# Last-keys operand of 96 rows, a theta tail of eight matmuls, softmax sums with a gap, and copies moved to ScalarE

## The chip, the cores and the metric

The kernel runs on one core of a Trainium2 chip. The metric is the device time of one execution in microseconds. Five engines have a queue of instructions each and run beside one another: TensorE (PE, with its weight loader PEld), VectorE (DVE), ScalarE (ACT), GpSimd (POOL) and SyncE (SP), which here issues the DMAs.

## The reference

```python
# attention: B, H, S, D = 8, 8, 576, 64; pool = 8; Sp = 72
k_p = k.reshape(B, H, Sp, pool, D).mean(axis=3)
v_p = v.reshape(B, H, Sp, pool, D).mean(axis=3)
scores = scale * np.matmul(q, k_p.transpose(0, 1, 3, 2))
scores = scores - np.max(scores, axis=-1, keepdims=True)
attn = np.exp(scores)
attn = attn / (np.sum(attn, axis=-1, keepdims=True) + 1e-09)
x = matmul(attn, v_p) -> (B, S, H * D)
# first mixer: x is (8, 576, 512)
theta = x @ w_theta
zr, zi = x * np.cos(theta), x * np.sin(theta)
y = einsum('ts,bsd->btd', w_tok_r, zr) + einsum('ts,bsd->btd', w_tok_i, zi)
u = x + y
x = u + np.maximum(u @ w_ch, 0.0)
# second mixer
h = np.maximum(x.transpose(0, 2, 1) @ w_tok1, 0.0) @ w_tok2
u = x + h.transpose(0, 2, 1)
out = u + np.maximum(u @ w_ch1, 0.0) @ w_ch2
```

## The kernel before

All is float32. Where a matmul runs in the float32r form, an operand is split into a hi part (a cast) and a lo part (what the cast lost), and hi·hi, hi·lo and lo·hi are added up in PSUM. PSUM has eight banks of 512 columns: two called m for the token mix, two called t for theta, four called x for scores, transposes and attention.

The prologue (to about 84 us) converts weights and does batch 0's attention. Then `interleave(mix_steps(b), side)` runs for b = 0 to 7: the token mix of batch b, 216 matmuls `m<-wtk,Z` in eight groups of 27, each group taken out by DVE at L789 (`R<-m,R`), and between them side steps for batch n = b + 1, the attention and theta that the next mix needs:

- `emit_sc`: scores, DVE's maximum (L552) and subtraction (L553), ACT's exp (L558);
- `emit_norm`, once for each of four pairs of heads p: DVE sums e (L564), adds 1e-9 and multiplies by 8 (L565), inverts (L568); POOL multiplies (L569) and copies the last eight of the 72 pooled keys of two heads into `pl` (L574);
- `emit_pt`: e transposed on PE (L173), 64 keys of two heads to a tile `pt`, the last eight keys of all heads to a tile `t`; ACT casts the hi part (L604, L608), DVE subtracts for the lo part (L605, L610);
- `emit_av`, for each of four pairs of heads j and two parts th of the tokens (256 and 320 columns): five matmuls into one x bank, three with `pt` (vbh, vbl, vbh) and two with the last keys (`vlh` of 128 rows and `vll`). ACT takes the result out twice (Xh L645, R L646), DVE subtracts (Xl L650);
- `dup_tail` (L536): the last 64 tokens of Xh, Xl and R (their chunk 4 is half full) are copied beside themselves, so that chunk 4 has 128 columns; the half that is copied gives the sine, the other the cosine;
- `emit_theta`: x @ w_theta into t banks, two halves (half) and chunks g; g = 2 is the tail, chunk 4, 12 matmuls of 512 columns (eight with Xh, four with Xl). ACT adds a constant that rounds (L705), DVE takes the fraction (L718), ACT takes the absolute value (L710, L714) and the sine (L711, L712, L715);
- `emit_z`: x transposed again, DVE multiplies (L736, L745), ACT casts (L750), POOL subtracts for the lo part (L751).

Keys, values and last values of later batches are loaded and summed in between: `prep_k` (sum over the pool of eight, L398, then two copies into the block-diagonal `bdk`, L403), `prep_v`, `prep_vl` (POOL builds vlh and vll from one 64-row sum by a mask).

The order is written by a planner: `mm` and `tp` count a clock of PE's columns, a table P gives each side step its due time on that clock within the mix, `later(dt, ...)` puts a follow-up dt behind, and `need` flushes what a tag still waits for. A scheduler then orders each engine's queue. So a matmul fewer shifts what is emitted where.

Of the kernel before, what the change touches and what calls it, by code (L numbers as in the profile page):

```python
# [64 lines left out]
def tile_attn_moe(  # L65
# [361 lines left out]
    def prep_vl(b):  # L427
        vr = vlr_t.pop(b)
        vs = st("vls", [128, 64], F32)
        vh = st("vlsh", [128, 64], F32R)  # L430
        nc.vector.tensor_reduce(
            out=vs, in_=vr.rearrange("p (d o) -> p d o", o=8), axis=AX.X, op=ALU.add
        )
        nc.scalar.copy(out=vh, in_=vs)
        m3 = mask.unsqueeze(2)

        def fin():
            nc.gpsimd.tensor_sub(out=vs, in0=vs, in1=vh.bitcast(F32))
# [6 lines left out]
            nc.gpsimd.tensor_tensor(
                out=vlo["l"][0:64].rearrange("p a e d -> p (a e) d"),
                in0=m3[0:64].to_broadcast([64, 8, 64]),
                in1=vs[0:64].unsqueeze(1).to_broadcast([64, 8, 64]),
                op=ALU.mult,
            )  # L450

        fin()
# [54 lines left out]
    def pool_vl(b):  # L507
        t, m = vn_t[b], pool_t[0]
        ps = bank_x()
        mm(ps, m[0:64, 192:320], t[0:64, 4], True, True)  # L510
# [7 lines left out]

# [5 lines left out]
        vll = vlo["l"]
        masked(tm, lo)
        masked(vlh, up)
        nc.scalar.copy(out=vlh[lo], in_=tm[lo])
        nc.gpsimd.tensor_sub(out=vll[lo], in0=tm[lo], in1=vlh[lo].bitcast(F32))
# [50 lines left out]
    def emit_pt(b, p):  # L579
# [36 lines left out]
    def emit_av(b, j, th):
        t0, n = TH[th]
        ts = slice(t0, t0 + n)
# [8 lines left out]
        if b == 0:  # L627
            keep_busy(ps, 2)
            mm(o, vb0[:, j, :], pt[:, ts], True, False)
            mm(o, vl0[0:64, j].rearrange("p e d -> p (e d)"), t1[0:64, ts], False, True)  # L630
# [45 lines left out]
    def emit_theta(b, half, g):  # L676
        if b == 0:
            cq_upto(8)
        else:
# [980 lines left out]
```

## Time and profile before

| | |
|---|---|
| median of 3 runs | 1313.01 us (1312.93 to 1313.25) |
| the profiled execution | 1310.61 us, span 1308.7 |
| PE busy | 1262.2 us, 96% of the span |
| DVE | 970.5 us, 74% |
| ACT | 637.1 us, 49% |
| POOL | 325.8 us, 25% |
| granted clock of PE | full speed in all 40 slices |

The span is what the trace covers; the execution has 1.9 us around it. Busy shares are averages over a prologue, eight mixes with side steps and the channel mix behind them.

### The profile page before, as it was taken

How to read it: one execution, taken by the hardware profiler on the slowest of the kernel's cores; microseconds unless marked ns; L12 is line 12 of the kernel's file. 1: busy time of each engine (PE TensorE's matmuls, PEld its weight loads, DVE VectorE, ACT ScalarE, POOL GpSimd, SP SyncE). 2: the span in 40 equal slices, each digit the busy share in tenths (PEclk: the TensorE clock that was granted, in tenths of full speed). 3: DMA queues.
4: the chain of work that ended last, by engine and by line, in shares of the span. 5: the costliest groups of instructions: out<-in, count | busy, mean ns of one | idle time of the engine just before them, and what ended most of it. 6: DMA issues, size and time to landing. Idle time of an engine off the chain costs nothing.

```text
span 1308.7 us, 22307 instructions
## 1 busy us (share of the span) xinstructions
PE 1262.2 (96%) x8216; PEld 1211.6 (93%) x8216; DVE 970.5 (74%) x1749; ACT 637.1 (49%) x1190; POOL 325.8 (25%) x340
## 2 busy tenths in 40 slices
PE   6899999999999998999999999999999999999998
PEld 3588999999999998999999998999999999999998
DVE  7988576675859598587765778897555499988894
ACT  4775455545555645243332346665445454444442
POOL 4653324242324244211110002320000031223122
PEclk9999999999999999999999999999999999999999
DMA  9423221222212123446684278885437976557621
GB/s 337 148 79 115 68 95 68 96 80 84 94 61 75 35 74 125 134 171 221 236 300 182 98 262 296 279 278 195 145 134 244 357 259 224 155 159 223 184 95 66
DMA packets 119612, 213.70 MB, mean 163 GB/s; under 512 B 11152, under 2 KB 65936, under 8 KB 119504
## 3 DMA queue, kind: packets, MB, share of 16 engines
q1 hardware_dynamic: 119504, 212.29, 48.3%
q8 instruction: 64, 1.05, 0.3%
q14 instruction: 44, 0.36, 0.1%
HBM read 133.60 MB, written 78.64 MB: 162 GB/s over the span
## 4 chain that ended last, share of the span: by engine, by line
PE 69%; DVE 20%; DMA 3%; issue 3%; ACT 2%; POOL 1%; SPq 0%; DVEq 0%; ACTq 0%; POOLq 0%
PE x L159 25%; PE m L159 21%; PE t L159 20%; PE x L173 2%; DVE sm L564 2%; DVE e L553 2%; DVE mx L552 2%; DVE tmp L736 1%; DVE sm L565 1%; DMA ws<-w_ch 1%; DVE pt L605 1%; DVE R L789 1%; DVE early L261 1%; DMA scr_x<-u 1%; DVE sums L398 1%
## 5 line engine op out<-in xcount | busy, mean ns | idle before, releaser
L159 PE MATMUL m<-wtk,Z 128*128 128x256 f32 (+1 forms) x1536 | 245.0, 298 | 8.4 <-DVE R L789 6.4
L159 PEld LDWEIGHTS m<-wtk,Z 128*128 128x128 f32 x1536 | 216.0, 188 | 11.5 <-DVE R L789 6.6
L751 POOL TENSOR_TENSOR Z<-tmp,Z 128x1024 fp32r<-128x1024 f32 x31 | 76.3, 2462 | 109.4 <-ACT Z L750 109.4
L159 PE MATMUL x<-ope_Z,wa 128*128 128x384 f32 x492 | 94.8, 336 | 0.0
L1382 POOL TENSOR_TENSOR o<-o,u 128x384 f32<-128x384 f32 x12 | 16.3, 1382 | 286.1 <-DVE u L1370 195.7
L159 PEld LDWEIGHTS x<-ope_Z,wa 128*128 128x128 f32 x492 | 86.3, 188 | 0.1
L1016 POOL TENSOR_TENSOR wsum<-wm 128x128 f32<-128x128 f32 (+1 forms) x18 | 15.1, 837 | 270.0 <-DVE wm L1006 262.4
L159 PE MATMUL t<-wth,Xh 128*128 128x256 f32 (+1 forms) x504 | 76.3, 293 | 0.5 <-DVE Xh L536 0.2
L159 PEld LDWEIGHTS t<-wth,Xh 128*128 128x128 f32 x504 | 66.9, 188 | 4.5 <-DVE Xh L536 1.8
L718 DVE SCALAR_TENSOR_TENSOR tmp<-tmp,t 128x512 f32<-128x512 f32 x40 | 27.3, 683 | 53.5 <-ACT tmp L705 53.5
L736 DVE TENSOR_TENSOR tmp<-x,tmp 128x1024 f32<-128x1024 f32 x32 | 39.1, 1220 | 31.2 <-ACT tmp L712 16.1
L159 PE MATMUL x<-bdk,q 128*128 128x144 f32 x320 | 47.8, 303 | 11.6 <-DVE bdk L1441 7.1
L159 PEld LDWEIGHTS x<-bdk,q 128*128 128x128 f32 x320 | 44.7, 204 | 13.9 <-issue 11.2
L159 PE MATMUL m<-wtk,zt 128*128 128x256 f32 (+1 forms) x192 | 56.6, 295 | 0.0
L705 ACT ACTIVATE tmp<-t,magic 128x512 f32<-128x512 f32 x40 | 27.3, 683 | 54.6 <-PE t L159 42.9
L569 POOL TENSOR_TENSOR e<-e,sm 128x720 f32<-128x720 f32 x32 | 45.0, 1406 | 31.6 <-DVE sm L568 31.1
L558 ACT ACTIVATE e<-e 128x720 f32<-128x720 f32 x32 | 25.7, 804 | 51.1 <-DVE e L553 51.0
L159 PE MATMUL t<-ope_Z,wa 128*128 128x384 f32 x234 | 48.1, 336 | 1.9 <-ACT p L1290 1.9
L789 DVE TENSOR_TENSOR R<-m,R 128x256 f32<-128x256 f32 (+1 forms) x64 | 28.7, 450 | 26.8 <-PE m L159 26.8
L159 PE MATMUL m<-ope_Z,wa 128*128 128x384 f32 x234 | 48.0, 336 | 0.0
L159 PE MATMUL x<-ope_R,wa 128*128 128x384 f32 x228 | 44.1, 338 | 0.3 <-DVE p L1295 0.2
L159 PE MATMUL t<-wth,Xl 128*128 128x256 f32 (+1 forms) x252 | 43.4, 294 | 0.0
(401 smaller groups left out, 3545.3 us busy)
## 6 DMA issues: line engine op xcount, KB each, us to landing
wa<-scr_w SPq DMA_DIRECT2D x42, 512.0 KB, 5.4
scr_g<-g SPq DMA_DIRECT2D x108, 192.0 KB, 2.9
scr_w<-wo SPq DMA_DIRECT2D x42, 256.0 KB, 3.0
scr_u<-R SPq DMA_DIRECT2D x32, 288.0 KB, 2.1
u<-scr_u SPq DMA_DIRECT2D x32, 288.0 KB, 3.9
scr_w<-wo SPq DMA_DIRECT2D x18, 512.0 KB, 3.4
scr_x<-u SPq DMA_DIRECT2D x32, 288.0 KB, 2.1
raw_n<-scr_x SPq DMA_DIRECT2D x24, 384.0 KB, 3.8
```

What stands on the lines that cost most here:

```text
L159: nc.tensor.matmul(out=o, lhsT=l, rhs=r, start=start, stop=stop, skip_group_check=skip)
L173: nc.tensor.transpose(o, i, ident)
L552: nc.vector.tensor_reduce(out=mx[:, c0:c1, :], in_=v, axis=AX.X, op=ALU.max)
L553: nc.vector.tensor_tensor(out=e[:, c0:c1, 2 * p:2 * p + 2, :], in0=v, in1=mx[:, c0:c1, :].unsqueeze(3).to_broadcast([128, n, 2, 72]), op=A ...
L558: nc.scalar.activation(out=ep, in_=ep, func=ACTF.Exp, scale=1.0 / 64.0)
L564: nc.vector.tensor_reduce(out=sm, in_=ep, axis=AX.X, op=ALU.add)
L569: nc.gpsimd.tensor_tensor(out=ep, in0=ep, in1=sm.unsqueeze(3).to_broadcast([128, 5, 2, 72]), op=ALU.mult)
L705: nc.scalar.activation(out=t, in_=pt, func=ACTF.Identity, bias=magic[:, 0:1])
L718: nc.vector.scalar_tensor_tensor(out=t, in0=t, scalar=MAGIC, in1=pt, op0=ALU.subtract, op1=ALU.subtract)
L736: nc.vector.tensor_tensor(out=tmp, in0=px.unsqueeze(1).to_broadcast([128, 2, 512]), in1=tmp, op=ALU.mult)
L751: later(1.0 if lo is nc.vector else 0.0, lambda: lo.tensor_sub(out=zl, in0=zv, in1=zh.bitcast(F32)), tg, zg)
L789: nc.vector.tensor_add(out=R[:, j, ts], in0=o, in1=R[:, j, ts])
```

## The change

- Last keys: `prep_vl`, `pool_vl`, `emit_pt` and `emit_av`. One operand of 96 rows takes the place of vlh and vll: rows 0 to 31 hold hi values, 32 to 63 lo values, 64 to 95 hi values again; against it two tiles t1 and n1 (four heads each) hold the weights as hi, hi, lo. Two loads of vl become six; batch 0 has one operand of 128 rows in place of 64.
- Theta tail: `dup_tail` no longer fills chunk 4 of Xh and Xl. A tile `xt` holds hi in columns 0 to 63 and lo in 64 to 127, and eight matmuls (hi and lo of w_theta, four k each) give both. ACT copies the lower half out, DVE adds (fold), and round, fraction, absolute value follow on 64 partitions.
- ACT, not DVE, copies xt (two) and R's tail, and `bdk` (L403).
- `emit_norm`: sums go to `ss`, a tile of 5 x 4 of which 5 x 2 are used; the scaling reads it and writes `sm`.

```diff
@@ prep_k
-            nc.vector.tensor_copy(
-                out=bdk[pr, 2 * g:2 * g + 2, 72 * e:72 * e + 72], in_=ks[pr]
-            )
+            nc.scalar.copy(out=bdk[pr, 2 * g:2 * g + 2, 72 * e:72 * e + 72], in_=ks[pr])
@@ prep_vl
+        for g in range(2):
+            nc.vector.tensor_reduce(
+                out=vs[0:96, g], in_=vr[g][0:96].rearrange("p (d o) -> p d o", o=8), axis=AX.X, op=ALU.add
+            )
+        nc.scalar.copy(out=vh[0:96], in_=vs[0:96])
+        nc.gpsimd.tensor_sub(out=vh[32:64], in0=vs[32:64], in1=vh[32:64].bitcast(F32))
+        m4 = mask[0:96, 0:4].unsqueeze(2)
+        for g in range(2):
             nc.gpsimd.tensor_tensor(
+                out=vlt[0:96, 2 * g:2 * g + 2].rearrange("p a e d -> p (a e) d"),
...
@@ emit_norm
+        ss = st(f"ss{p % 2}", [128, 5, 4], F32)[:, :, 0:2]
         sm = st(f"sm{p % 2}", [128, 5, 2], F32)
-        nc.vector.tensor_reduce(out=sm, in_=ep, axis=AX.X, op=ALU.add)
+        nc.vector.tensor_reduce(out=ss, in_=ep, axis=AX.X, op=ALU.add)
         nc.vector.tensor_scalar(
-            out=sm, in0=sm, scalar1=1e-9, scalar2=8.0, op0=ALU.add, op1=ALU.mult
+            out=sm, in0=ss, scalar1=1e-9, scalar2=8.0, op0=ALU.add, op1=ALU.mult
         )
@@ emit_pt, p == 4
-                nc.scalar.copy(out=pt[:, t0:t0 + n], in_=ps[:, 0:n])
-                lo = pt[64:128, t0:t0 + n]
+                for g in range(2):
+                    gr = slice(64 * g, 64 * g + 32)
+                    nc.scalar.copy(out=pt[g][0:64, t0:t0 + n], in_=ps[64 * g:64 * g + 64, 0:n])
+                    later(P["lo"], lambda o=pt[g][64:96, t0:t0 + n], i=ps[gr, 0:n], h=pt[g][0:32, t0:t0 + n]:
+                          nc.vector.tensor_sub(out=o, in0=i, in1=h.bitcast(F32)),
@@ emit_av
-            (vlh[:, j].rearrange("p e d -> p (e d)"), t1[:, ts]),
-            (vlo["l"][:, j].rearrange("p e d -> p (e d)"), t1[:, ts]),
+            (vlt[0:96, j].rearrange("p e d -> p (e d)"), t1[j // 2][0:96, ts]),
...
-                dup_tail(h)
-                dup_tail(l)
-                dup_tail(r)
+                for a, x in enumerate((h, l)):
+                    nc.scalar.copy(out=xt[b][:, :, a], in_=x[:, :, 512:T].bitcast(F32))
+                dup_tail(r, nc.scalar.copy)
@@ emit_theta, tail = g == 2 and b > 0
+                for w in range(2):
+                    for k in range(4):
+                        mm(o, xt[b][:, k].rearrange("p a t -> p (a t)"), wth[k][:, w, d0:d0 + nd],
+                           n == 0, n == 7)
...
+            lo = tmp[0:64, 0, :]
+            nc.scalar.copy(out=lo, in_=pt[64:128])
+            def fold():
+                th = tmp[64:128, 0, :]
+                nc.vector.tensor_add(out=th, in0=pt[0:64], in1=lo)
+                nc.scalar.activation(out=t[64:128], in_=th, func=ACTF.Identity, bias=magic[64:128, 0:1])
+                def frac():
+                    nc.vector.scalar_tensor_tensor(
+                        out=t[64:128], in0=t[64:128], scalar=MAGIC, in1=th, op0=ALU.subtract, op1=ALU.subtract
```

In the changed kernel the lines move: L565 is L553, L564 is L552, L610 is L599, L650 is L640, L718 is L740 (L713 in the tail), L789 is L811.

DVE's queue from the last norm to the last keys of n = 3, before (sm are the softmax sums, pt and t the transposed weights, R what the mix adds to):

```order
L565 TENSOR_SCALAR sm_2295<-sm_2295 128x10
L398 TENSOR_REDUCE sums<-kr 128x144
L568 RECIPROCAL sm_2295<-sm_2295 128x10
L605 TENSOR_TENSOR pt_2355<-x_2356,pt_2355 128x256
L605 TENSOR_TENSOR pt_2355<-x_2360,pt_2355 128x320
L403 COPY bdk<-sums 64x2x72 x2
L605 TENSOR_TENSOR pt_2372<-x_2373,pt_2372 128x256
L410 TENSOR_REDUCE sums<-vr 128x128
L605 TENSOR_TENSOR pt_2372<-x_2378,pt_2372 128x320
L789 TENSOR_TENSOR R_1731<-m_2342,R_1731 128x320
L610 TENSOR_TENSOR t_2403<-x_2404,t_2403 64x256
L610 TENSOR_TENSOR t_2403<-x_2408,t_2403 64x320
```

And in the changed kernel:

```order
L553 TENSOR_SCALAR sm_2312<-ss_2311 128x10
L408 TENSOR_REDUCE sums<-vr 128x128
L556 RECIPROCAL sm_2312<-sm_2312 128x10
L592 TENSOR_TENSOR pt_2377<-x_2378,pt_2377 128x256
L592 TENSOR_TENSOR pt_2377<-x_2382,pt_2377 128x320
L592 TENSOR_TENSOR pt_2394<-x_2395,pt_2394 128x256
L592 TENSOR_TENSOR pt_2394<-x_2400,pt_2394 128x320
L811 TENSOR_TENSOR R_1751<-m_2364,R_1751 128x320
L599 TENSOR_TENSOR t_2425<-x_2427,t_2425 32x256
L599 TENSOR_TENSOR t_2426<-x_2427,t_2426 32x256
L599 TENSOR_TENSOR t_2425<-x_2432,t_2425 32x320
L599 TENSOR_TENSOR t_2426<-x_2432,t_2426 32x320
```

The bdk copies and one reduction ahead of the pt subs are gone from here, and two t subs have become four, of 32 partitions.

PE's queue in the last of these AV groups and the start of the theta tail of n = 3, before (x and t name banks, m the mix's bank, wth the theta weights):

```order
L159 MATMUL x_2526<-pt_2481,vbh 128x320
L159 MATMUL x_2526<-pt_2481,vbl 128x320
L159 MATMUL x_2526<-pt_2481,vbh 128x320
L159 MATMUL x_2526<-t_2403,vlh 128x320
L159 MATMUL x_2526<-t_2403,vll 128x320
L159 MATMUL m_2396<-wtk_552,Z_2076 128x256
L159 MATMUL m_2396<-wtk_559,Z_2076 128x256
L159 MATMUL m_2396<-wtk_594,zt_1879 128x256
L159 MATMUL m_2543<-wtk_473,Z_2076 128x320
L159 MATMUL m_2543<-wtk_481,Z_2076 128x320
L159 MATMUL m_2543<-wtk_493,Z_2076 128x320
```

In the changed kernel, the same AV group and what follows it:

```order
L159 MATMUL x_2555<-pt_2512,vbh 128x320
L159 MATMUL x_2555<-pt_2512,vbl 128x320
L159 MATMUL x_2555<-pt_2512,vbh 128x320
L159 MATMUL x_2555<-t_2426,vlh 128x320
L159 MATMUL m_2528<-wtk_521,Z_2089 128x320
L159 MATMUL m_2528<-wtk_556,Z_2089 128x320
L159 MATMUL m_2528<-wtk_563,Z_2089 128x320
L159 MATMUL m_2528<-wtk_598,zt_1902 128x320
L159 MATMUL m_2528<-wtk_477,Z_2089 128x320
```

The last keys take one matmul, not two. Between this AV group and the tail, 16 matmuls of the mix stand in the changed queue where 15 stood; the tail is eight `t_2592<-wth,xt` where it was twelve.

ACT's queue from the last AV copies to the theta tail of n = 3, before:

```order
L645 CAST Xh<-x_2526 128x320
L646 COPY R_2414<-x_2526 128x320
L424 CAST vbh<-sums 64x2x64
L434 CAST vlsh<-vls 128x64
L705 ACTIVATE tmp_2578<-t_2563,magic 128x512
L714 ACTIVATE tmp_2578<-tmp_2578 64x512
L715 ACT_TABLE_LOAD
L715 ACTIVATE tmp_2578<-tmp_2578,phase 128x512
L705 ACTIVATE tmp_2609<-t_2581,magic 128x512
```

In the changed kernel:

```order
L636 COPY R_2440<-x_2555 128x320
L643 CAST xt<-Xh 128x4x64
L523 COPY R_2440<-R_2440 128x4x64
L422 CAST vbh<-sums 64x2x64
L643 CAST xt<-Xl 128x4x64
L422 CAST vbh<-sums 64x2x64
L433 CAST vlsh<-vls 96x128
L705 COPY tmp_2603<-t_2592 64x512
L710 ACTIVATE tmp_2603<-tmp_2603,magic 64x512
L727 ACTIVATE tmp_2634<-t_2606,magic 128x512
L718 ACTIVATE tmp_2603<-tmp_2603 64x512
L719 ACT_TABLE_LOAD
```

The three tail copies stand between the last R copy and the tail, two vbh casts among them, and the tail has a copy ahead of its rounding; the rounding of the next chunk (tmp_2634) now comes before the tail's absolute value.

## Rows read from the trace of the kernel before

**Rows 1.** Busy us by stretch: length, PE, PEld, DVE, ACT, POOL, clock, DMA share, GB/s.

```profile
200.00:240.00 40.00, 38.76 (x304) 38.06 (x304) 30.53 (x61) 19.51 (x37) 15.55 (x16) 1.00 0.26 87
480.00:520.00 40.00, 36.27 (x272) 34.70 (x271) 33.09 (x81) 21.86 (x44) 16.12 (x13) 1.00 0.32 96
```

**Rows 2.** What PE waited for, 150:450 (total, times, longest, us).

```profile
PE m L159 <- DVE R L789: 4.2, 5, 0.9
PE x L159 <- DVE t L610: 1.5, 5, 0.3
PE x L159 <- DVE pt L605: 0.8, 5, 0.2
```

**Rows 3.** Timeline of PE, n = 3 (start, us, engine, line, operation, idle before).

```profile
240.43 0.28 PE L159 MATMUL x<-t,vll 128*128 128x256 f32 x1
240.55 0.31 PE L159 MATMUL x<-pt,vbh 128*128 128x320 f32 x1
...
242.00 0.40 PE L159 MATMUL m<-wtk,Z 128*128 128x256 f32 x2
...
244.35 2.12 PE L159 MATMUL t<-wth,Xh 128*128 128x512 f32 x8
246.31 1.07 PE L159 MATMUL t<-wth,Xl 128*128 128x512 f32 x4
247.21 1.10 PE L159 MATMUL t<-wth,Xh 128*128 128x256 f32 x8
```

**Rows 4.** Timeline of POOL and DVE in the scores of n = 3 and 4.

```profile
217.70 2.38 POOL L751 TENSOR_TENSOR Z<-tmp,Z 128x1024 fp32r<-128x1024 f32 x1 [2.48 <-ACT Z L750]
217.97 2.13 DVE L565 TENSOR_SCALAR sm<-sm 128x10 f32<-128x10 f32 x1
...
278.07 2.15 DVE L565 TENSOR_SCALAR sm<-sm 128x10 f32<-128x10 f32 x1
```

**Rows 5.** DVE groups by line and form, 150:450 (busy, mean ns | idle before).

```profile
L565 DVE TENSOR_SCALAR sm<-sm 128x10 f32<-128x10 f32 x20 | 13.1, 656 | 0.0
...
L403 DVE COPY bdk<-sums 64x144 f32<-64x144 f32 x20 | 8.7, 433 | 0.1
...
L536 DVE CAST Xh<-Xh 128x256 fp32r<-128x256 f32 x5 | 3.4, 677 | 0.0
...
L610 DVE TENSOR_TENSOR t<-x,t 64x320 fp32r<-64x320 f32 x5 | 2.4, 486 | 0.0
```

**Rows 6.** What PE waited for, 90:130 (n = 1), first of five.

```profile
PE x L173 <- POOL e L569: 1.0, 1, 1.0
```

**Rows 7.** What PE waited for, 450:515 (n = 7).

```profile
PE m L159 <- DVE R L789: 1.8, 2, 1.5
PE m L159 <- POOL Z L751: 1.8, 1, 1.8
PE x L159 <- DVE t L610: 1.4, 1, 1.4
```

**Rows 8.** ACT groups by line and form, 150:450.

```profile
L424 ACT CAST vbh<-sums 64x128 fp32r<-64x128 f32 x20 | 6.0, 298 | 0.4
...
L608 ACT CAST t<-x 128x320 fp32r<-128x320 f32 x5 | 2.1, 426 | 0.0
```

**Rows 9.** Timeline of theta and z behind it, n = 3.

```profile
248.13 0.69 DVE L718 SCALAR_TENSOR_TENSOR tmp<-tmp,t 128x512 f32<-128x512 f32 x1 [0.94 <-ACT tmp L705]
...
248.86 0.63 ACT L714 ACTIVATE tmp<-tmp 64x512 f32<-64x512 f32 x1 [0.76 <-DVE tmp L718]
...
261.39 1.05 ACT L750 CAST Z<-tmp 128x1024 fp32r<-128x1024 f32 x1 [1.29 <-DVE tmp L736]
...
266.37 0.86 PE L159 MATMUL m<-wtk,Z 128*128 128x256 f32 x6
```

**Rows 10.** Timeline of the weight loader (PEld) in the prologue.

```profile
40.24 0.29 PEld L159 LDWEIGHTS x<-t,vl 64*128 64x128 f32 x2 [0.33 <-issue]
...
40.86 0.11 PEld L169 LDWEIGHTS <-busy 128*128 128x128 bf16 x2 [0.33 <-issue]
```

More of the change, by code (lines that the diff above doesn't have):

```diff
@@ L364, in open_vlo @@
         vlo["b"] = st("vbl", [128, 4, 128], F32R)
-        vlo["l"] = st("vll", [128, 4, 2, 64], F32R)
-        for t in vlo.values():
-            nc.gpsimd.memset(t.bitcast(F32), 0.0)
+        nc.gpsimd.memset(vlo["b"].bitcast(F32), 0.0)
     q_t = {}
@@ L389, in load_vl @@
     def load_vl(b):
-        t = st("vlr", [128, 512], F32)
-        nc.sync.dma_start(out=t[0:64], in_=vl[b])
-        nc.sync.dma_start(out=t[64:128], in_=vl[b])
+        t = [st(x, [128, 512], F32, "vlr") for x in ("vlr", "n2")]
+        for g in range(2):
+            for r in range(3):
+                nc.sync.dma_start(out=t[g][32 * r:32 * r + 32], in_=vl[b, 32 * g:32 * g + 32])
         vlr_t[b] = t
@@ L428, in prep_vl @@
         vr = vlr_t.pop(b)
[L429 to L438, printed above, removed]
+        vs = st("vls", [128, 2, 64], F32)
+        vh = st("vlsh", [128, 2, 64], F32R)
+        for g in range(2):
[6 more added lines that the diff above has]
+        for g in range(2):
             nc.gpsimd.tensor_tensor(
-                out=vlh.rearrange("p a e d -> p (a e) d"),
-                in0=m3.to_broadcast([128, 8, 64]),
-                in1=vh.bitcast(F32).unsqueeze(1).to_broadcast([128, 8, 64]),
+                out=vlt[0:96, 2 * g:2 * g + 2].rearrange("p a e d -> p (a e) d"),
+                in0=m4.to_broadcast([96, 4, 64]),
+                in1=vh[0:96, g].bitcast(F32).unsqueeze(1).to_broadcast([96, 4, 64]),
                 op=ALU.mult,
             )
[L445 to L452, printed above, removed]
     kn_t = {}
@@ L511, in pool_vl, with masked @@
         v = ps.rearrange("p (h d) -> p h d", h=8)
-        def masked(o, pr):
+        def masked(o, pr, m):
             nc.vector.tensor_tensor(
                 out=o[pr].rearrange("p a e d -> p (a e) d"), in0=v[pr],
-                in1=mask[pr].unsqueeze(2).to_broadcast([64, 8, 64]), op=ALU.mult,
+                in1=m[pr].unsqueeze(2).to_broadcast([pr.stop, 8, 64]), op=ALU.mult,
             )
-        lo, up = slice(0, 64), slice(64, 128)
         if b == 0:
-            masked(vl0, lo)
+            masked(vl0, slice(0, 128), mask0)
             return
         tm = st("kr", [128, 4, 2, 64], F32, "vlt")
[L524 to L528, printed above, removed]
+        masked(tm, slice(0, 96), mask)
+        nc.scalar.copy(out=vlt[0:96], in_=tm[0:96])
+        nc.gpsimd.tensor_sub(out=vlt[32:64], in0=tm[32:64], in1=vlt[32:64].bitcast(F32))
     e_t = {}
@@ L574, in emit_norm @@
             nc.gpsimd.tensor_copy(
-                out=pl_t[b][:, :, :, 2 * p + h, :],
+                out=pl_t[b][:, :, p // 2, :, 2 * (p % 2) + h, :],
                 in_=left.unsqueeze(2).to_broadcast([128, 5, 2, 8]),
@@ L584, in emit_pt @@
         else:
-            pt = st("t1", [128, T], F32R if b else F32)
-            t1_t[b] = pt
+            t1_t[b] = [st(x, [128, T], F32R, "t1") for x in ("t1", "n1")] if b else st("t1", [128, T], F32)
+            pt = t1_t[b]
         for c0, c1 in ((0, 2), (2, 5)):
@@ L599, in emit_pt @@
             if b == 0:
-                o, i = (pt[:, t0:t0 + n], ps[:, 0:n]) if p < 4 else (pt[0:64, t0:t0 + n], ps[0:64, 0:n])
-                (nc.scalar.copy if c0 else nc.vector.tensor_copy)(out=o, in_=i)
+                (nc.scalar.copy if c0 else nc.vector.tensor_copy)(out=pt[:, t0:t0 + n], in_=ps[:, 0:n])
             elif p < 4:
@@ L679, in emit_theta @@
         else:
-            need("Xl")
+            need("Xl", "n3")
         chunks, d0, nd = theta_geo(half, g)
+        tail = g == 2 and b > 0
         if g < 2:
@@ L704, in emit_theta, with sins @@
         t = tmp[:, 1, :]
+        if tail:
+            lo = tmp[0:64, 0, :]
[7 more added lines that the diff above has]
+                        out=t[64:128], in0=t[64:128], scalar=MAGIC, in1=th, op0=ALU.subtract, op1=ALU.subtract
+                    )
+                    def sins():
+                        nc.scalar.activation(out=t[0:64], in_=t[64:128], func=ACTF.Abs)
+                        nc.scalar.activation(out=t, in_=t, func=ACTF.Sin, scale=-TWO_PI, bias=phase[:, 1:2])
+                    later(P["sn"], sins, tg)
+                later(P["fr"], frac, tg)
+            later(P["sn"], fold, bk, tg)
+            return
         nc.scalar.activation(out=t, in_=pt, func=ACTF.Identity, bias=magic[:, 0:1])
```

32 lines of the change are left out of this document (20 added, 12 removed).

## The prediction

> **What bounds the kernel now.** I read the stretches first. In 200:240 TensorE (PE) is busy 38.76 of 40 us, VectorE (DVE) 30.53, ScalarE (ACT) 19.51 and GpSimd (POOL) 15.55, all at the full granted clock [rows 1]: this part of the program runs at the rate at which PE takes matmuls, so a matmul fewer is time saved, and what remains is the little that PE waits. In 480:520 PE has 36.27: there something else ends last. The long DVE instruction L565 comes back in the same place after 60.1 us, from 217.97 to 278.07 [rows 4]: that is one batch, and 150 to 450 holds the steady ones, n = 2 to 6 (n is the batch whose attention runs beside the mix of batch n-1). Then the waits of PE in 150:450: 4.2 us behind R L789 in five times, 1.5 behind t L610 in five, 0.8 behind pt L605 in five [rows 2], or 0.84 + 0.30 + 0.16 = 1.3 us a batch. The waits at either end: n = 1 has five, together 2.6 us, the longest 1.0 behind POOL's e [rows 6], and n = 7 has 1.8 behind R L789, 1.8 behind Z L751 and 1.4 behind t L610, together 5.0 [rows 7]. Behind the mix of batch 6 nothing differs: from the mix of batch 7 on (about 513 us) the change's instructions are the same, in the same order, on all five engines. All 796 us that follow cancel out.
>
> **Matmuls removed (13.7 us).** The pace [rows 3]: a matmul of 256 columns starts 0.12 us before the next (240.43 to 240.55). From 240.55 to 242.00 ten of 320 columns take 1.45, so 0.145 each. The four of 512 columns with Xl take 0.90 (246.31 to 247.21), so 0.225 each; the eight before them 0.245 each. Each batch n of 1 to 7 loses eight matmuls with vll, four of 256 and four of 320 columns: 4 x 0.12 + 4 x 0.145 = 1.06 us. It loses the four with Xl in the theta tail: 0.90. Sum 1.96 a batch, 13.7 for seven. None lies beside other PE work, so all of it is on the path wherever PE is never short of data: n = 2 to 6, and most of n = 1.
>
> **The wait on POOL (4.2 us).** At 217.70 POOL starts Z L751, 2.38 us; at 217.97 DVE starts L565, 10 columns, and takes 2.13: both end at 220.1, 0.02 us apart [rows 4]. Twenty L565 take 13.1 us [rows 5], 2.62 a batch; without the long one's 2.13, the other three have 0.16 each. So 2.13 - 0.16 = 1.97 us a batch are waiting. All the DVE queue stands behind it: the norms of the other three head pairs, then R L789, for which PE waits 0.8 us later. The new L553 reads from a tile with gaps and still writes without. I take the wait as gone, with 0.16 for L553, as the other three L565 have it. DVE is then 2 us earlier, the 0.84 goes, and PE's next limit there is itself: 5 x 0.84 = 4.2. Bounds: 0 if the stall stays, and 4.2.
> The Trainium skill, page "VectorE: DVE Perf Modes", section "What auto-detection actually checks", says a one-source operation takes the two-port mode when the outermost dimensions of source and destination are both even or equal. "SBUF — State Buffer", section "Who interferes with whom", says that such an operation and a GpSimd instruction shut each other out for the whole instruction. The 0.02 us between the two ends agree with the second. By the first, 10 against 10 locks, and 5 (with a gap) against 10 does not, if the destination is taken as one run of ten; taken as 5 by 2 on both sides it would lock as before, which is the first rival.
>
> **The bdk copies and dup_tail leave DVE (0.75 us).** L403 is 20 x 433 ns, 1.74 a batch with its waiting; the three copies of L536 are 677 + 282 + 281 ns by their groups, of which rows 5 show the first, near 1.2 a batch. DVE gets in exchange two more t subs (0.9 for the pair: one of 64 partitions and 320 columns takes 0.49 [rows 5], and 32 partitions have the same columns), a second 0.69 us reduction, and a fold of 64 x 512 of about 0.69 by the L718 row [rows 9]. Net: 1.97 + 1.74 + 1.24 - 2.3 = 2.7 us less of 60, and earlier by more than that where pt L605 stands: 0.15 x 5 = 0.75 us. Bounds 0 and 0.8. The wait behind t L610 I leave as it is: four casts instead of two now stand on ACT ahead of its subs, which gives back what DVE gains. Bounds 1.5 saved, and 1.5 lost if the second pair of casts (0.43 for 320 columns [rows 8]) comes late.
>
> **ACT takes it on (nothing, but see xt).** Four bdk copies of about 0.3, two more t casts of 0.4, three copies of 0.37 and one of 0.63 add 3.7 us to some 29 in 60 (19.51 of 40 [rows 1]), so 55%. The theta tail's chain grows by ACT's copy (0.63) and DVE's fold (0.69) and shrinks by 0.90 of matmuls; a copy of 64 x 512 is taken at nearly the 128 x 512 time. From the tail's first matmul to PE's next mix there are 22.0 us (244.35 to 266.37), and the last Z it needs is cast by 262.44 [rows 3, 9]. 3.9 us of slack, less 0.9 that PE arrives earlier and 0.4 of chain, leave 2.6: no wait. SP issues six loads of vl a batch where two stood, ahead of those for q, k and v of later batches, and POOL builds the operand in two shorter passes, not two long ones; no wait of PE in 150:450 ends with a DMA or with POOL [rows 2], so both cost nothing, and would cost what a late operand costs if the loads, a batch ahead, were late by a whole batch.
>
> **xt (1.4 us lost).** Xh's last 64 tokens used to be copied by DVE (0.68 us [rows 5]). Now PE needs both xt copies before the first of eight tail matmuls. The last four AV groups take 8 x 0.12 + 8 x 0.145 and two mix matmuls, 2.4 us; ACT evacuates each with two copies, about 0.3 each from start to start, so that its last is done near 3.4. Then DVE's Xl sub (0.49), R's copy, one vbh cast (0.30 [rows 8]) and xt's lo half stand in line: ready at about 4.75 us from the first AV, where PE, with 16 mix matmuls of 0.145 in between, comes at 4.7. Bounds 0 and 0.9 a batch; I take 0.2, seven times 1.4, near the covered end because the order leaves those 16 matmuls there.
>
> **The ends (1.5 us).** n = 1: of 2.6 us, the ones behind DVE's norm and POOL's e go with an L565 that is long there too; I take 1.5 (bounds 0 and 2.6). n = 7: DVE works through weight conversions there (33.09 of 40 us [rows 1]) and R L789 queues among them; of its 5.0 us I take nothing, and count its 1.96 of matmuls in full. Bounds -2.0 (matmuls saved, waited for instead) and +5.0. Prologue: eight 64-row matmuls become 128-row. The weight conversions on DVE set the time there, so nothing; bounds 0 and 2.4, 0.3 for each pair.
> What a change of height costs: the weight loads of the 64*128 pair, and those behind it, begin with 0.33 us of idle time [rows 10]. The new rows are 96 high, which no row shows.
> The Trainium skill, page "TensorEngine Tiling (Array Packing)", section "Key Properties", says that changing the tiling mode drains the engine; the 0.33 us agree. The page lists heights of 32, 64 and 128; by it 96 rows run in the mode of 128 and cost nothing, and the sum would stay.
>
> **The sum.** 13.7 + 4.2 + 0.75 - 1.4 + 1.5 = 18.75. The profiled execution is 1310.61 us (span 1308.7 and 1.9 around it), 0.18% under the median of the runs, 1313.01. A span of 1290.0 and, against the median, 1313.0 - 18.75 = 1294.3.
>
> **Rivals.**
> 1. The waits stay (the gap does not free L553, or another instruction takes the place of the stall): 13.7 - 1.4 + 0 of the rest, 1300.7. For it: PE waits at the same places although DVE has 9 us of 40 spare, so order, not load, makes them. Against: the earliest cause of each is a row of 2.1 us.
> 2. ACT becomes the chain: xt late by 0.9 in each batch, and the t casts 0.3 later. 1294.3 + 7 x 0.7 + 5 x 0.3 = 1300.7, the same by another place. For it: ACT runs two copies per AV group, and AV is now shorter. Against: the 16 matmuls ahead of the tail.
> 3. The 96-row operands break PE's row mode as 64 rows do: 8 groups in 7 batches, 56 excursions. One switch is 0.33 us [rows 10], there and back 0.66. Up to 37 us: 1294.3 + 56 x 0.33 = 1312.8 to 1331.3, 1322 in the middle. It decides from 0.335 an excursion, where 18.75 us are used up. Against: 96 rows need all the rows that 128 need.
> 4. The end of n = 7 gives way too: DVE, 2.7 us lighter, clears 5.0 of waits: 1294.3 - 5.0 = 1289.3. Against: the conversions, not the attention, fill its queue, and they stay.
>
> **Chances.** Forecast 0.55 (1291 to 1298), rival 1 0.15, rival 2 0.12, rival 4 0.12, rival 3 0.03, rest 0.03. If all bounds fall well, 13.7 + 4.2 + 0.8 + 1.5 + 2.6 + 5.0 + 2.4 = 30.2, so 1282.8; if all badly, 13.7 - 6.3 - 1.5 - 2.0 = 3.9, so 1309.1. For 8 in 10 I take 1288 to 1302.5: rivals 1, 2 and 4 lie inside, and the far ends need several bounds at once. A measurement of this kernel can tell 0.2%, 2.6 us, from no change. Faster by more: all cases but rival 3 and a part of the rest, 0.95; rival 3 splits between the same, 0.02, and slower, 0.03.
>
> **What would show it.** In the changed trace: L553 at 160 ns throughout and PE's wait behind R L811 gone (right), or one of 2 us in each batch (rival 1). PE's first tail matmul t<-wth,xt with an idle time before it (rival 2; over 0.5 us a batch refutes my 0.2). Rows of 96*128, with idle loads beside them or starts 0.12 and 0.145 apart (rival 3 or not). The period between two L553 of the same place: 60.1 - 1.96 - 0.84 - 0.15 + 0.2 = 57.35 us. The waits at 474 to 511, still 5 us or less (rival 4). The forecast is wrong as a whole if the period stays above 59, or the part from 513 us on differs in length.

## The result and the profile after

The changed kernel takes 1298.61 us (median of 4 runs, 1297.42 to 1301.13), the kernel before 1312.97 beside it: ratio 0.9895, interval 0.9877 to 0.9912, so 14.4 us less where 18.75 were forecast. On another chip it was 1300.21 against 1314.16, ratio 0.9889 (0.9872 to 0.9907). The profiled execution takes 1297.42 us, span 1295.6. It lies 1.2 us under the median of its runs, the profiled execution of the kernel before (1310.61) 2.4 us under its own; so the two spans differ by 13.1 us only.

The times of stages come from the traces: the start of the last matmul `m<-wtk` of each token mix. The mix of batch b ends where n = b + 1 has its attention behind it. "A batch" is the mean of mixes 1 to 5 (n = 2 to 6), the last column what is left of the span.

| kernel | to the end of mix 0 | a batch | mix 6 (n = 7) | mix 7 | rest |
|---|---|---|---|---|---|
| before | 143.51 | 60.04 | 60.43 | 39.27 | 765.3 |
| before, a second profile (e11) | 145.76 | 60.03 | 60.59 | 39.24 | 766.1 |
| changed | 141.86 | 56.85 | 59.92 | 40.01 | 769.6 |
| changed, a second profile (e7) | 142.13 | 56.86 | 60.99 | 41.21 | 769.8 |
| before with the gap alone (e1) | 143.12 | 58.56 | 60.02 | 39.75 | 769.1 |
| changed, sums in place (e2) | 141.85 | 58.13 | 60.29 | 39.60 | 767.2 |
| changed, copies on DVE (e9) | 142.06 | 56.78 | 59.43 | 40.69 | 770.4 |
| changed, lo of n = 7 on DVE (e8) | 143.21 | 56.86 | 59.55 | 35.77 | 770.0 |
| before, lo of n = 7 on DVE (e14) | 142.28 | 60.11 | 59.85 | 36.17 | 768.0 |

So the steady batches gave 3.19 us each, 16.0 for five, more than the 2.75 forecast. The beginning gave 1.65, the end of the stage with n = 7 nothing (0.5 gained in mix 6, 0.7 lost in mix 7), and the rest, where nothing was to change, is 4.3 us longer. A batch is the same in both profiles of either kernel within 0.01 us; the other columns differ by up to 2.3 us between two profiles of one kernel.

The stretches of the changed kernel, with the columns of [rows 1]; the first is the prologue's end:

```profile
40.00:80.00 40.00, 32.02 (x139) 23.61 (x138) 35.67 (x69) 28.54 (x64) 28.00 (x31) 0.87 0.46 151
200.00:240.00 40.00, 39.96 (x307) 39.16 (x306) 30.29 (x65) 24.73 (x55) 15.97 (x18) 1.00 0.29 97
440.00:480.00 40.00, 39.13 (x296) 37.92 (x295) 39.00 (x105) 25.10 (x58) 18.70 (x22) 1.00 0.24 77
480.00:520.00 40.00, 35.38 (x258) 34.85 (x258) 26.14 (x46) 15.46 (x25) 13.82 (x10) 0.96 0.30 101
```

PE is busy 39.96 of 40 us where it was 38.76 [rows 1]. In 440:480 DVE is the one nearly without a gap, 39.00 of 40. In 480:520 PE's granted clock is 0.96, where the kernel before had 1.00 [rows 1].

POOL and DVE in the scores of n = 3, the place of [rows 4]:

```profile
213.72 2.40 POOL L773 TENSOR_TENSOR Z<-tmp,Z 128x1024 fp32r<-128x1024 f32 x1 [3.00 <-ACT Z L772]
213.89 0.15 DVE L553 TENSOR_SCALAR sm<-ss 128x10 f32<-128x10 f32 x1
```

The scaling starts 0.17 us after POOL's Z (0.27 before) and takes 0.15 us beside it. By the Trainium skill, page "VectorE: DVE Perf Modes", section "What auto-detection actually checks", outermost dimensions of 5 and 10 are neither both even nor equal, so the two-port mode is off, if the destination is taken as one run of ten; the 0.15 us agree. The groups of DVE, to be set against [rows 5]:

```profile
L599 DVE TENSOR_TENSOR t<-x,t 32x320 fp32r<-32x320 f32 x10 | 4.9, 486 | 0.3
...
L709 DVE TENSOR_TENSOR tmp<-t,tmp 64x512 f32<-64x512 f32 x5 | 3.4, 684 | 1.6 <-ACT tmp L705 1.5
L553 DVE TENSOR_SCALAR sm<-ss 128x10 f32<-128x10 f32 x20 | 3.1, 153 | 0.0
```

L553's twenty take 3.1 us in place of 13.1. A t sub of 32 partitions takes the 486 ns of one with 64, as assumed, and the fold 684. PE in the last AV groups and the tail of n = 3, beside [rows 3]:

```profile
235.47 0.30 PE L159 MATMUL x<-pt,vbh 128*128 128x320 f32 x1
235.61 0.31 PE L159 MATMUL x<-t,vlh 96*128 96x320 f32 x1
235.76 0.31 PE L159 MATMUL x<-pt,vbh 128*128 128x320 f32 x1
...
238.70 2.09 PE L159 MATMUL t<-wth,xt 128*128 128x512 f32 x8
240.63 1.11 PE L159 MATMUL t<-wth,Xh 128*128 128x256 f32 x8
```

The 96-row matmul starts 0.14 after its neighbour and is followed after 0.15, the pace of the 128-row ones, with no idle time. The tail's eight take 1.93 us (238.70 to 240.63), where twelve took 2.86. In 150:440 no wait of PE is long enough to be listed; [rows 2] had 6.5 us. What is left is in 440:505, in the place of [rows 7]:

```profile
PE m L159 <- ACT Z L772: 3.0, 1, 3.0
PE m L159 <- DVE R L811: 1.6, 1, 1.6
PE x L159 <- DVE t L599: 0.9, 1, 0.9
```

5.5 us, where there were 5.0; the forecast's sign was 5 or less.

### The profile page after: what moved, and what is told of

Read it like the earlier page. It is cut to its first block, busy times and chain, and to the rows that moved or that the text cites. A ratio compares the mean times of both kernels' runs of the same rounds, so it can differ in the third digit from the quotient of the medians.

```text
span 1295.6 us, 22271 instructions
## 1 busy us (share of the span) xinstructions
PE 1254.6 (97%) x8130; PEld 1209.8 (93%) x8132; DVE 956.9 (74%) x1730; ACT 661.0 (51%) x1256; POOL 321.9 (25%) x339
## 4 chain that ended last, share of the span: by engine, by line
PE 76%; DVE 9%; DMA 2%; issue 2%; ACT 2%; POOL 0%; SPq 0%; ACTq 0%; DVEq 0%; POOLq 0%
PE m L159 28%; PE x L159 25%; PE t L159 19%; PE x L173 3%; DMA ws<-w_ch 1%; DMA scr_x<-u 1%; DVE wm L1024 1%; DVE raw_n L1155 1%; DVE wm L1028 1%; DVE wsum L1039 0%; DVE p L1313 0%; DVE g L1323 0%; ACT wo L1052 0%; DVE ope_R L1152 0%; ACT wm L1018 0%
## 5 line engine op out<-in xcount | busy, mean ns | idle before, releaser
L159 PE MATMUL m<-wtk,Z 128*128 128x256 f32 (+1 forms) x1536 | 253.6, 301 | 4.6 <-ACT Z L772 3.0
L159 PEld LDWEIGHTS m<-wtk,Z 128*128 128x128 f32 x1536 | 220.2, 190 | 6.1 <-ACT Z L772 3.2
L159 PE MATMUL t<-wth,Xh 128*128 128x256 f32 x448 | 62.9, 282 | 0.0
L159 PEld LDWEIGHTS t<-wth,Xh 128*128 128x128 f32 x448 | 57.9, 188 | 0.9 <-DVE tmp L709 0.2
L159 PEld LDWEIGHTS x<-bdk,q 128*128 128x128 f32 x320 | 44.5, 203 | 13.1 <-issue 10.9
L740 DVE SCALAR_TENSOR_TENSOR tmp<-tmp,t 128x512 f32<-128x512 f32 x33 | 22.5, 683 | 31.3 <-ACT tmp L727 31.3
L811 DVE TENSOR_TENSOR R<-m,R 128x256 f32<-128x256 f32 (+1 forms) x64 | 28.8, 450 | 20.2 <-PE m L159 20.2
L772 ACT CAST Z<-tmp 128x1024 fp32r<-128x1024 f32 x32 | 33.4, 1043 | 20.0 <-DVE tmp L758 20.0
L159 PE MATMUL m<-ope_Xl,wa 128*128 128x384 f32 x204 | 42.9, 338 | 0.6 <-ACT ope_Xl L1151 0.6
```

Of the source, the lines that this page charges most:

```text
L159: nc.tensor.matmul(out=o, lhsT=l, rhs=r, start=start, stop=stop, skip_group_check=skip)
L740: nc.vector.scalar_tensor_tensor(out=t, in0=t, scalar=MAGIC, in1=pt, op0=ALU.subtract, op1=ALU.subtract)
L772: nc.scalar.copy(out=zh, in_=zv)
L811: nc.vector.tensor_add(out=R[:, j, ts], in0=o, in1=R[:, j, ts])
```

## The experiments

**e1, the gap alone**, in the kernel before:

```diff
+        ss = st(f"ss{p % 2}", [128, 5, 4], F32)[:, :, 0:2]
         sm = st(f"sm{p % 2}", [128, 5, 2], F32)
-        nc.vector.tensor_reduce(out=sm, in_=ep, axis=AX.X, op=ALU.add)
+        nc.vector.tensor_reduce(out=ss, in_=ep, axis=AX.X, op=ALU.add)
         nc.vector.tensor_scalar(
-            out=sm, in0=sm, scalar1=1e-9, scalar2=8.0, op0=ALU.add, op1=ALU.mult
+            out=sm, in0=ss, scalar1=1e-9, scalar2=8.0, op0=ALU.add, op1=ALU.mult
```

> The kernel before with one edit: the softmax sums go to the tile with gaps, and the scaling reads it. Theory 1 (the wait of VectorE on GpSimd is what delays R L789, and with it TensorE): L565's successor takes 0.16 us everywhere, TensorE's wait of 0.84 us behind R goes in n = 2 to 6 and a part of n = 1 with it: 1305.5 to 1308.5 us. Rival (the waits went because copies left VectorE, the gap did little): 1311 to 1313 us, with the waits behind R still there.

1307.96 us, ratio 0.9954 (0.9939 to 0.9969), 6.2 us less. A batch takes 58.56, 1.48 less, and no wait of PE is listed in 150:450, though all copies still stand on DVE. One group of DVE in it, over 150:450:

```profile
L566 DVE TENSOR_SCALAR sm<-ss 128x10 f32<-128x10 f32 x20 | 3.1, 154 | 0.0
```

Theory 1 holds, and more came of it than it said: the waits behind t L610 and pt L605 went with the one behind R.

**e2, sums in place**, the reverse edit in the changed kernel.

> The changed kernel with the sums back in place, without a gap. Theory 1: the scaling takes 2.1 us once a batch, and TensorE's wait behind R comes back with 0.84 us in five batches: 1301.5 to 1303.5 us. Rival (VectorE is now light enough to hide 2 us): the 2.1 us are there, but TensorE does not wait, 1298 to 1299.6 us.

1300.94 us, ratio 0.9896 (0.9876 to 0.9915), a little under the 1301.5 that theory 1 expected at least. Its total can't be told from the changed kernel's, but its stages can: a batch takes 58.13, 1.28 more, and PE's waits in 150:440 are

```profile
PE m L159 <- DVE R L810: 6.8, 5, 1.4
```

6.8 us in five. DVE without the copies does not hide the stall. The total shows less than these 6.4 us: the two profiled executions differ by 4.0, since the rest of the program is 2.4 us shorter than in the changed kernel (below, e7), and runs differ by some us in their stretches at half clock.

**e9, copies on DVE**, in the changed kernel:

```diff
-            nc.scalar.copy(out=bdk[pr, 2 * g:2 * g + 2, 72 * e:72 * e + 72], in_=ks[pr])
+            nc.vector.tensor_copy(out=bdk[pr, 2 * g:2 * g + 2, 72 * e:72 * e + 72], in_=ks[pr])
...
-                    nc.scalar.copy(out=xt[b][:, :, a], in_=x[:, :, 512:T].bitcast(F32))
-                dup_tail(r, nc.scalar.copy)
+                    nc.vector.tensor_copy(out=xt[b][:, :, a], in_=x[:, :, 512:T].bitcast(F32))
+                dup_tail(r)
```

> The changed kernel with the bdk copies, both xt copies and R's tail back on VectorE. Theory 1 (the gap alone took the waits of the steady batches away, VectorE has time to spare there): the period stays at 56.85 us, and only the ends may lose: 1298 to 1300 us. Rival (moving the copies is worth what the prediction gave it, 0.15 us a batch and more): period 57.0 to 57.6, 1300 to 1303 us.

1299.51 us, ratio 0.9893 (0.9876 to 0.9909); a batch takes 56.78. Moving the copies to ACT is worth nothing here.

**e7, the changed kernel again**, on the chip of e8 to e10.

> The changed kernel once more, beside the kernel before on the same chip, for the size of the gain and for the pace of the channel mix. Theory: the 3 us by which the stretch from 900 us on was longer in the changed kernel's profile is a state of the run (all its matmuls 1 ns apart more), not the change: the ratio is 0.987 to 0.989, and the median gain 14 to 16 us. Rival (the change slows the channel mix): every run of it shows the slower pace, and the gain stays at 14 or less.

Ratio 0.9889, in the theory's range, but the theory falls: this profile has the slower pace too, as have all ten profiles of kernels with the gap (changed, e1, e3, e4, e7 to e10, e12, e13), and none of the four without (before, e2, e11, e14). Stretches of the channel mix where PE is never idle, first before, then e2, e1 and the changed kernel, placed where each is at the same matmuls:

```profile
1100.00:1200.00 100.00, 100.00 (x577) 100.00 (x576) 85.51 (x97) 44.24 (x58) 26.42 (x20) 1.00 0.63 196
```

```profile
1091.00:1191.00 100.00, 100.00 (x577) 100.00 (x576) 84.84 (x97) 44.17 (x58) 24.97 (x20) 1.00 0.64 196
```

```profile
1094.80:1194.80 100.00, 100.00 (x572) 100.00 (x571) 83.91 (x97) 44.06 (x58) 26.34 (x20) 1.00 0.63 194
```

```profile
1085.60:1185.60 100.00, 100.00 (x572) 100.00 (x572) 82.72 (x97) 43.98 (x58) 26.48 (x20) 1.00 0.63 194
```

577 matmuls in 100 us without the gap, 572 with it. Over 1100 to 1290 the mean step from matmul to matmul is 0.1740 and 0.1752 us. PE's 4560 matmuls behind mix 7 are the same ones in the same order in both. The step does not go up alike for all: of 1100 of them (the 3301st to the 4400th behind mix 7), 63 have a step of 179 ns or more in the kernel before and 157 in the changed one. From 900 us to the end the pace makes 2.5 us. The gap's tile is all that e1 adds, so the edit brings the pace with it; what in it PE notices, such as where other tiles come to lie, was not tried.

**e8, the lo of Z on DVE for n = 7**, in the changed kernel:

```diff
-        for g, t0, t1, lo in zip((2, 0, 1), P[f + "th0"], P[f + "z0"], (nc.gpsimd,) * 3):
+        for g, t0, t1, lo in zip((2, 0, 1), P[f + "th0"], P[f + "z0"], (nc.vector if n == B - 1 else nc.gpsimd,) * 3):
```

> The changed kernel; in n = 7 alone the three subtractions for the lo part of Z (half 0) are on VectorE, not GpSimd. Theory 3 (the end of n = 7 is set by a VectorE queue that is busy without a gap and locked three times behind GpSimd's Z, 1.1 + 2.2 + 1.8 us): 3.1 us of work more, 5.1 of waiting less, TensorE's waits of 1.6 behind R and 3.0 behind Z shrink by 1 to 2 us: 1296.5 to 1298 us. Rival (the work, not the locks, sets the end): VectorE gets 3.1 us more, and TensorE waits longer: 1300 to 1302 us.

1293.59 us, ratio 0.9843 (0.9828 to 0.9859): 6.6 us less than e7 beside it, and more than the theory expected (1296.5 at the least). What it takes away, in the changed kernel first, POOL, DVE and PE at the end of n = 7:

```profile
482.81 2.54 POOL L773 TENSOR_TENSOR Z<-tmp,Z 128x1024 fp32r<-128x1024 f32 x1 [1.16 <-ACT Z L772]
...
483.00 2.47 DVE L249 TENSOR_SCALAR cvt<-stg 128x192 uint32<-128x192 uint32 x1
...
489.67 1.65 PE L159 MATMUL m<-wtk,Z 128*128 128x256 f32 x6 [2.98 <-ACT Z L772]
489.70 2.57 POOL L773 TENSOR_TENSOR Z<-tmp,Z 128x1024 fp32r<-128x1024 f32 x1 [2.84 <-ACT Z L772]
...
490.34 2.13 DVE L296 TENSOR_TENSOR wk2a<-cvt,wk2a 128x192 fp32r<-128x192 f32 x1
```

Two small conversions, L249 and L296 of 192 columns, each stand for over 2 us beside POOL's Z. In e8, the same lines of DVE:

```profile
483.21 1.21 DVE L773 TENSOR_TENSOR Z<-tmp,Z 128x1024 fp32r<-128x1024 f32 x1
...
485.54 0.25 DVE L249 TENSOR_SCALAR cvt<-stg 128x192 uint32<-128x192 uint32 x1
...
489.41 1.22 DVE L773 TENSOR_TENSOR Z<-tmp,Z 128x1024 fp32r<-128x1024 f32 x1
490.54 0.35 DVE L296 TENSOR_TENSOR wk2a<-cvt,wk2a 128x192 fp32r<-128x192 f32 x1
```

Z's subtraction takes 1.21 on DVE, and the conversions 0.25 and 0.35. PE's waits of e8 in 435:515, of which the 3.0 behind Z is gone; the granted clock over 480:520 is 1.00:

```profile
PE m L159 <- DVE R L811: 1.5, 2, 1.2
PE x L159 <- DVE t L599: 0.9, 1, 0.9
```

The Trainium skill, page "SBUF — State Buffer", section "Who interferes with whom", says that a VectorE operation with two SBUF inputs meets GpSimd's reads as well; L296, with two, agrees with 2.13 us.

**e14, the same edit in the kernel before.**

> The kernel before with e8's edit alone (lo of Z of n = 7 on VectorE). Theory 3 (the end of n = 7 was limited by VectorE's queue and its locks before the change too, so the change's matmuls could not shorten it): 3 to 6 us less than before, 1308 to 1311. Rival (only the changed kernel's end is limited there): within 1.5 us of the kernel before.

1309.01 us, ratio 0.9964 (0.9950 to 0.9978), 6.0 less. Mix 7 takes 36.17 in place of 39.27. Mixes 6 and 7 give 3.7 of the 6.0. The end of n = 7 was held up there before the change too, as theory 3 says. But the edit does two things at once: it ends the standstill of the conversions beside POOL's Z, and it makes the subtraction itself shorter (1.21 in place of 2.5), and one of PE's waits before was behind POOL's Z itself (1.8 [rows 7]). How much each gives is not separated.

**e12 and e13**: e8 with the lo of mix 7's own half on DVE too (`(nc.vector if b == B - 1 else nc.gpsimd,) * 2` in the z1 list), and e8 with e9's copies.

> As e8, and the lo subtractions of batch 7's other half (in its own mix) on VectorE too. VectorE has idle time there (26 of 40 us busy in 480:520), and GpSimd's 2.4 us become 1.2: if these Z are waited for, 1 to 2 us less than e8 (1292 to 1293.5); if not, the same within 1 us; slower by 1 to 2 us if the subtractions stand ahead of conversions that the next stage waits for.

> As e8, with the bdk copies, xt and R's tail on VectorE. Theory 1 and 3: nothing in the steady batches; at the end of n = 7, where VectorE has no gap, the copies (about 2.4 us in that batch) push the conversions back: 0 to 2 us slower than e8. Rival (moving the copies to ScalarE is worth nothing anywhere): same as e8 within 0.7 us.

1293.81, ratio 0.9839 (0.9824 to 0.9855), and 1292.78, ratio 0.9834 (0.9819 to 0.9848): both the same as e8, so there is nothing in the further Z, and the copies cost DVE nothing at the end of n = 7 either. All three beat both kernels; the plainest is e8.

**e11, the kernel before once more**, unchanged.

> The kernel before, for one more profile. Theory: the profile that the prediction read was one of its luckiest runs (granted clock 1.000 from start to end, the faster of two paces in the channel mix); another profile of the same kernel shows stretches at half clock before 80 us and near 500, and with the slower pace 3 us more behind 900 us: 1311 to 1317 us. Rival (the kernel before keeps its clock, and the changed one loses it): clock 1.000 again.

1313.54 us, clock 0.995. The prologue's end in it, beside the same stretch of the profile that the prediction read:

```profile
40.00:80.00 40.00, 34.68 (x152) 24.40 (x153) 38.86 (x74) 30.33 (x67) 25.01 (x32) 0.96 0.40 141
```

```profile
40.00:80.00 40.00, 33.94 (x157) 23.65 (x156) 39.20 (x75) 31.05 (x68) 26.20 (x32) 1.00 0.40 141
```

Granted clock 0.96 here and 1.00 there; 19 runs of the kernel before on the chip of e1 to e4 lie at 0.992 to 0.997. So the half clock in the prologue is not the change's, and the profile read was of a lucky run. The expectation was wrong in two places: near 500 us e11 keeps its clock (1.00 over 480:520), and its pace is the faster one.

**e3, e10 and e4, on the half clock in the prologue.** e3 and e10 put fillers ahead of batch 0's theta tail (ten of `rhs=r_t[0][:, 3, 0:512]`, twenty of `rhs=pt_t[0, 3][:, 320:576]`, both with `lhsT=ident`), e4 gives batch 0's last keys 64 rows:

```diff
-            mm(o, vl0[:, j].rearrange("p e d -> p (e d)"), t1[:, ts], False, True)
+            gr = slice(64 * (j // 2), 64 * (j // 2) + 64)
+            mm(o, vl0[gr, j].rearrange("p e d -> p (e d)"), t1[gr, ts], False, True)
```

> The changed kernel with ten filler matmuls (identity by R, overwritten after) ahead of batch 0's theta tail, where TensorE sits idle for 5.8 us before its clock is at half. Theory 2 (the longer idle time in the prologue costs the clock, and that eats a part of the gain): no stretch at half clock near 52 to 60, the 18 matmuls take 5.7 in place of 7.4 us; if the second one near 76 goes too, 1295 to 1297 us. Rival (VectorE sets the prologue's end anyway, the clock costs nothing): 1298.6 us within 0.7, whatever the clock.

> The changed kernel with 20 filler matmuls of 256 columns (identity by batch 0's last transposed weights, overwritten after) between the last attention matmul of batch 0 and its theta, where TensorE idles 5.8 us. The filler of e3 waited for R and came after the idle time. Theory 2 (idle time there brings the half clock, and that costs about 1.7 us): about 4.4 us of the idle time filled, no half clock at 52 to 60, end of the first mix 1 to 2 us sooner than 141.9: 1296.5 to 1298 us. Rival (VectorE sets the end of the prologue): the mix ends at the same place within 0.5 us.

> The changed kernel in which batch 0's last-keys matmuls use 64 rows again (rows 0 to 63 or 64 to 127 by head pair, same result). Theory 2: TensorE comes to the idle place about 2.4 us later, idles 3.3 us as before, keeps its clock: 1295.5 to 1298 us. Rival (the 128 rows are a gain, as they save 0.3 us eight times): 1298.6 to 1301 us.

1313.10 (ratio 0.9996, 0.9981 to 1.0011), 1312.73 (0.9990, 0.9978 to 1.0003) and 1298.49 (0.9882, 0.9862 to 0.9903). e3 and e10 miss all that was expected of them, and e4 lies between its two ranges. The fillers tell nothing of the clock: they changed what stands where in DVE's queue, and PE then waits there. Of e10's PE:

```profile
49.27 8.80 PE L681 MATMUL t<-pt,con 128*128 128x256 f32 x40
57.91 7.05 PE L159 MATMUL t<-wt,R 128*128 128x512 f32 x24
...
78.18 5.77 PE L159 MATMUL t<-wt,R 128*128 128x256 f32 x16 [12.78 <-DVE tmp L743]
```

8.8 us of fillers, twice the length meant, then 12.8 us of waiting for DVE. e4's idle time was 3.1 us, as in the kernel before, and its trace still has stretches at 1.2 GHz near 63 and 77 us (granted clock 0.92 over 40:80). So theory 2, that the longer idle time costs the clock, falls in that form.

## Why the prediction was right, and where its steps were not

- **Matmuls, 1.96 a batch**: measured 1.71 (58.56 in e1 to 56.85). The tail's four gave 0.93 for 0.90. The last keys gave the remaining 0.78 for 1.06. About half of what is missing lies in longer steps at the matmuls of 256 columns, too short for PE's list of waits (the mean step to a last-keys matmul is 0.183 us, in e1 0.152; the weight loader still waits for the t subs, 1.4 us in five batches, in e1 1.0); where the other half lies is not shown. Mis-sized by an eighth.
- **The wait on POOL, 0.84 a batch**: right in mechanism, too small. The gap alone gives 1.48, since t L610 and pt L605 were late for the same 2 us. The forecast had left the first as it was and given the second to the copies.
- **The copies, 0.15 a batch**: nothing, by e9.
- **ACT**: no wait in 150:440. The chain and the bounds of the theta tail held.
- **xt, 0.2 lost a batch**: no wait listed in 150:440; the 16 mix matmuls cover it.
- **96 rows (rival 3)**: no price; the loader's only idle time before the forty of 150:440 is those 1.4 us behind DVE's t. On the page "TensorEngine Tiling (Array Packing)" of the Trainium skill, section "Key Properties", a drain comes with a change of mode; no run here shows one at 96 rows. That 96 rows run in the mode of 128 is the prediction's own conclusion from the heights listed there; the page doesn't speak of 96.
- **n = 1 and the prologue, 1.96 + 1.5 less 0.2**: 1.65 against the profile that was read, 3.9 against e11. The two profiles of before differ by 2.25 at that place, so the size isn't settled.
- **n = 7, "count its 1.96 of matmuls in full"**: this step failed. The bound of -2.0 beside it was the right end, but its reason ("waited for instead") covers a small part: mixes 6 and 7 together took 99.9 us where they took 99.7, and PE's waits in them rose only from 5.1 to 5.5 us. In mix 7 one wait of 3.0 behind Z stands where two of 1.5 and 1.8 stood, and as PE goes on after it its granted clock falls:

```profile
488.00:492.00 4.00, 2.33 (x11) 2.33 (x12) 4.00 (x10) 1.67 (x3) 2.30 (x1) 0.69 0.36 119
```

The kernel before has 1.00 there. e10 has the same wait of 3.0 with its clock at 1.00 over 480:520, and its mix 7 takes 39.12 in place of 40.01; e7, at 0.91, takes 41.21. So of the 2.0 that are missing about 1 is the clock's and 0.3 are waits; the rest is not placed. The wait of 3.0 comes from DVE's queue: its multiply stands behind the 2.47 us of L249 (above), and ACT's cast waits for it:

```profile
487.33 1.21 DVE L758 TENSOR_TENSOR tmp<-x,tmp 128x1024 f32<-128x1024 f32 x1
488.58 1.04 ACT L772 CAST Z<-tmp 128x1024 fp32r<-128x1024 f32 x1 [2.44 <-DVE tmp L758]
```

In e8 mixes 6 and 7 go from 99.9 to 95.3 us: PE's waits from 5.5 to 2.3, and the half clock is gone with the long one. In e14, the kernel before, they go from 99.7 to 96.0.
- **After 513 us, "all 796 us that follow cancel out"**: this step failed too, by 4.3 us. The order is the same, but 2.5 us from 900 us on are the pace that all kernels with the gap have (e7). Another 1.0 is a transfer, and not the change's. ACT's wait for the weights `ws`, and PE's wait behind it, before:

```profile
556.97 0.66 ACT L996 ACTIVATE wm<-ws 128x512 f32<-128x512 f32 x1 [3.16 <-DMA ws<-w_ch]
...
559.73 0.44 PE L173 MATMUL x<-con,u 128*128 128x128 f32 x2 [0.22 <-DVE u L878]
```

and in the changed kernel:

```profile
540.58 0.67 ACT L1018 ACTIVATE wm<-ws 128x512 f32<-128x512 f32 x1 [4.16 <-DMA ws<-w_ch]
...
543.35 0.44 PE L173 MATMUL x<-con,u 128*128 128x128 f32 x2 [1.22 <-DVE u L900]
```

ACT waits a us longer for the load, and PE 1.22 in place of 0.22. But the kernel before has this too in its second profile (e11), and e1, which has the gap, does not (PE 0.27):

```profile
560.19 0.67 ACT L996 ACTIVATE wm<-ws 128x512 f32<-128x512 f32 x1 [4.12 <-DMA ws<-w_ch]
...
562.96 0.44 PE L173 MATMUL x<-con,u 128*128 128x128 f32 x2 [1.18 <-DVE u L878]
```

The remaining 0.8 is not placed.

Together: 16.0 (five batches) + 1.65 - 0.2 (mixes 6 and 7) - 4.3 = 13.1, the difference of the spans. The time lies inside the stated range, but above the 1291 to 1298 of the forecast itself. That it comes so near is in part luck: the steady batches gave 2.2 us more than their sum, and the others 7.9 less: 1.6 at the beginning, 2.0 at n = 7 and 4.3 behind it. By the prediction's own last sign, a part behind 513 us that differs in length, the forecast does not hold as a whole; what holds is the account of the steady batches, with a period of 56.85 where 57.35 was forecast.

## What to carry to other kernels

A long instruction of ten columns beside a GpSimd instruction that ends at the same time is a place to look: a layout with a gap, in one small tile, took 1.5 us from every batch, while the copies that were moved between engines moved nothing. Matmuls saved where another engine's queue ends last gave nothing here, and in most profiles TensorE's clock fell behind the one long wait that took the place of two shorter ones; count saved matmuls only in stretches in which TensorE waits for nothing. And a second profile of the kernel before tells which part of a stage's time is the run's and not the kernel's.

## What the hardware showed that was not expected

- A matmul of 384 columns steps by 0.1740 or 0.1752 us in the mean through the end of the channel mix, with the same matmuls in the same order, TensorE never idle and its clock at 1.00: four profiles of four without the gap's tile, ten of ten with it. The cause was not tried.
- TensorE's clock in the prologue. Where it idled before the first theta matmuls, the 18 records behind it went by at 2.4 GHz in the kernel before and in part at 1.2 in the changed one:

```profile
55.55 5.86 PE L159 MATMUL t<-wt,R 128*128 128x512 f32 x18 [3.09 <-DVE R L536]
```

```profile
55.88 7.61 PE L159 MATMUL t<-wt,R 128*128 128x512 f32 x18 [5.77 <-DVE R L523]
```

5.86 us after 3.1 us of idle time, 7.61 after 5.8. But e4 and e11 have stretches at 1.2 GHz near 63 us with 3.1 us of idle time there as well.
- TensorE's clock in mix 7. Seven profiles have a wait of 2.9 or 3.0 us behind Z there: over 480:520 the granted clock is 0.91 to 0.96 in six of them (changed, e2, e3, e4, e7, e9) and 1.00 in e10. e8 and e12 to e14, without that wait, have 1.00. But e1 has 0.96 with no wait over 1.5 us, and the kernel before, with 1.5 and 1.8, has 1.00; so the wait alone does not decide it.
